# The last 3072 tokens of a pooled attention and feed-forward kernel: h for 768 tokens at a time from seven products of a 2x2 split, with w_in's combined weights made on VectorE and kept in DRAM

## The chip, the cores and the metric

The kernel runs on one core of a Trainium2 chip. The time is that of the device, in microseconds, from the start to the end of one execution. TensorE (PE) multiplies matrices and loads its weights (PEld) beside them; VectorE (DVE), ScalarE (ACT) and GpSimd (POOL) work element by element; SyncE (SP) issues the copies between DRAM and the on-chip memory.

## The reference

```python
def _attn_ref(q, k, v):                       # q, k, v: 8 batches, 8 heads, 576 tokens, 64
    k_p = k.reshape(B, H, 72, 8, D).mean(axis=3)
    v_p = v.reshape(B, H, 72, 8, D).mean(axis=3)
    scores = np.matmul(q, k_p.transpose(0, 1, 3, 2)) / np.sqrt(D)
    attn = np.exp(scores - scores.max(-1, keepdims=True))
    attn = attn / (attn.sum(-1, keepdims=True) + 1e-09)
    return np.matmul(attn, v_p)

def _moe_ref(x, w_in, w_out):                 # x: 4608 x 512, w_in: 512 x 2048, w_out: 2048 x 512
    h = x @ w_in
    g = h * np.clip(h + 3.0, 0.0, 6.0) / 6.0
    return g @ w_out
```

x is the attention's result, its heads side by side. All of it is in float32.

## The kernel before

**Precision.** A float32 number is kept as the sum of two numbers of a shorter format (`hi`, a rounded copy, and `lo`, what is left), and a product is three matmuls: hi by hi, lo by hi, hi by lo. So x, g, w_in, w_out, the attention weights and the pooled values all exist in two parts. Weights are scaled by 2^8 on the way.

**Blocks.** The 4608 tokens are worked on in blocks of 512, 256, 384, six times 512, and 384 tokens (`BLOCKS`). d_ff is cut into 16 slices f of 128. For a block, a `Step` for each f does:

- `h` (L775, matmuls L782): 12 matmuls, 4 slices of d_model by 3 products, as wide as the block, into one of two PSUM banks h0 and h1;
- `relu` (ScalarE, L790), `gate` (VectorE, L794, reads the bank again), `hi` (ScalarE, L798) and `lo` (VectorE, L802) make g in two parts;
- `out` (matmuls L812): for each 128 tokens three matmuls of 512 columns into the banks o0 to o3, which add up over all f. After the last f each bank is scaled, copied out and stored (L818, L819).

`run` (L1004) goes through the 16 steps of a block with a lag of two: `h` of step u, then `out` of step u-2. So between h of a step and its out, TensorE has two other h and two other out.

**Attention** for a block is a list of small steps (`block_steps`, L609): scores of a tile of 128 tokens and 4 heads (matmul L412, maximum L416 on VectorE, four exps L420 on ScalarE, division L448 and L454 on GpSimd), transposes (L518, L520) and the product with the pooled values (`av`, matmuls L583), whose result ScalarE copies to x (L585). Loads of q, k, v and the pooling of k and v (L214, L332, on VectorE) hang on these steps. `Paced.slot` hands out the steps of the next block between the matmuls of this one, so that x is complete before the next block begins; `split_x` (L556) then makes x's two parts.

**Order.** The tile framework derives the waits from what each instruction reads and writes. The order on each engine from the first load to the fourth step of block 1 is written out by hand (`ORDER`). Behind it a planner orders each engine's instructions when the program is built: first in the program comes first, among those that are ready in its own timeline. Engines then work in that fixed order, and so does SP's queue of copies.

**Weights.** All of w_in and w_out are loaded and split once during block 0 (`Prep`) and stay in the on-chip memory: 16 tiles w_f, each with w_in and w_out of one f in two parts.

Of the kernel before, what the change touches and what calls it, by code (L numbers as in the profile page):

```python
# [17 lines left out]
P = 128  # L18
# [3 lines left out]
BLOCKS = [512, 256, 384] + [512] * 6 + [384]  # L22
# [5 lines left out]

WSCALE = 2.0**8

# [45 lines left out]
def attention_moe_kernel(  # L76
# [50 lines left out]
    const = ctx.enter_context(tc.tile_pool(name="const", bufs=1))  # L127
    pool = ctx.enter_context(tc.tile_pool(name="pool", bufs=2))
    psum = ctx.enter_context(tc.tile_pool(name="psum", bufs=1, space=PSUM))

# [46 lines left out]
    def stage(i):  # L177

        if i % 2 == 0:
            stages.append(const.tile([P, 2, 2 * DM], F32, name="stage", tag=f"w_{NF - 2 - i // 2}"))  # L180
        return stages[-1][:, i % 2]
# [187 lines left out]
    def load_second():  # L369

        t = const.tile([P, 2, 2 * DM], F32, name="v1", tag=f"w_{NF - 2 - 6}")
# [172 lines left out]

    xs = {}

    def x_tile(j, name, dtype):
        if (j, name) not in xs:
            xs[j, name] = pool.tile([P, NCC, max(BLOCKS)], dtype, name=name, bufs=1)
        return xs[j, name][:, :, : BLOCKS[j]]  # L550

# [83 lines left out]
    w_in_hi, w_in_lo, w_out_hi, w_out_lo = {}, {}, {}, {}  # L635
    wraw, ubuf = {}, []
# [5 lines left out]
    def w_tile(name, f, a, b, shape, dtype):  # L642
        tag = f"w_{f}" if (a, b) == (0, 2) else f"w_{f}_{a}"
        return const.tile([P, b - a] + shape, dtype, name=f"{name}_{f}", tag=tag)
# [10 lines left out]
    class Prep:  # L655
# [10 lines left out]
        def __init__(self, f):  # L666
            self.f, self.made = f, {}
            if f < 2:
                ubuf.append(const.tile([P, 2 * DM], F32, name="u", tag=f"w_{NF - 1}_{1 - f}"))
# [34 lines left out]
        def place(self, part, n):  # L704

            f, (a, b, _, _) = self.f, part
            if a not in self.made:
                x, y = next(g for g in groups(f) if g[0] <= a < g[1])
                w = w_tile("w", f, x, y, [2, DM], F32R)
                for i in range(x, y):  # L710
                    self.made[i] = w, i - x
                    for m in range(2):
                        t = w[:, i - x, m]
# [35 lines left out]
    class Block:  # L749
# [3 lines left out]
        def sums(self, t):  # L753

            if t not in self.pos:
                banks = [self.banks[t]]
                if self.j == len(BLOCKS) - 1 and t == self.nt - 1:
                    banks.append(self.banks[t + 1])
                n = DM // len(banks)
                self.pos[t] = [  # L760
                    (slice(i * n, (i + 1) * n), psum.tile([P, DM], F32, name="pso", tag=b)[:, :n])
                    for i, b in enumerate(banks)
                ]
            return self.pos[t]
# [4 lines left out]
    class Step:  # L769
# [18 lines left out]
        def relu(self):  # L788
            self.g = pool.tile([P, max(BLOCKS)], F32, name="g", bufs=1)[:, : self.n]
# [6 lines left out]
        def hi(self):  # L796
            self.ghi = pool.tile([P, max(BLOCKS)], F32R, name="ghi", bufs=3)[:, : self.n]
            nc.scalar.copy(self.ghi, self.g)  # L798

        def lo(self):  # L800
            self.glo = pool.tile([P, max(BLOCKS)], F32R, name="glo", bufs=3)[:, : self.n]
            nc.vector.tensor_tensor(out=self.glo, in0=self.g, in1=self.ghi.bitcast(F32), op=ALU.subtract)  # L802

        def out(self, slot=no_slot, tiles=None):
            f, blk = self.f, self.blk
            for t in tiles or range(self.t0, self.t1):
# [3 lines left out]
                for cols, pos in blk.sums(t):  # L810
                    for i, (l, r) in enumerate(products):
                        nc.tensor.matmul(pos, l, r[:, cols], start=f == 0 and i == 0, stop=f == NF - 1 and i == 2)  # L812
# [4 lines left out]
                for (cols, pos), scaled in zip(blk.sums(t), (nc.scalar.mul, nc.vector.tensor_scalar_mul)):  # L817
                    scaled(o[:, cols], pos, 1.0 / WSCALE**2)  # L818
                    nc.sync.dma_start(out[at : at + P, cols], o[:, cols])  # L819


    ident = const.tile([P, P], F32, name="ident")
    make_identity(nc, ident)
    small = const.tile([P, 7], F32, name="small")
    mask, half = small[:, :6], small[:, 6:]
    nc.gpsimd.memset(half, 0.5)
    kbds = [const.tile([P, NPAIR, 2 * SP], F32, name=f"kbd{i}") for i in range(2)]
# [3 lines left out]
    nc.gpsimd.memset(half, 0.5)  # L831

    class Paced:


        def __init__(self, steps, n):
            self.steps, self.n, self.at, self.done = steps, n, 0, 0

# [4 lines left out]
        def upto(self, m):  # L843
            while self.done < m:
# [4 lines left out]
                if step:  # L849
                    step()  # L850

# [118 lines left out]
    def att_steps(j):  # L970

        if j == len(BLOCKS):
            return []
# [30 lines left out]
    def run(steps, lag, attention, first_slot=0, preps={}):  # L1004


        n_out = sum(x.t1 - x.t0 for x in steps[max(first_slot - lag, 0) : len(steps) - lag])
        paced = Paced(attention, len(steps) - first_slot + n_out - 4)
        for u in range(len(steps) + lag):
# [25 lines left out]
            if steps[0].blk.j == 1 and u == 3:  # L1035
                window.append(len(traced))
            if u == len(steps) - 1:
                paced.upto(len(attention))
                if attention:
                    split_x(steps[0].blk.j + 1)  # L1040
            if u >= len(steps) and steps[0].blk.j == len(BLOCKS) - 1:
                continue
            if u >= lag:
                steps[u - lag].out(slot)
        if steps[0].blk.j < len(BLOCKS) - 1:
            return

        mark = len(traced)
        for tiles in range(steps[0].blk.nt - 1), [steps[0].blk.nt - 1]:
            for x in steps[len(steps) - lag :]:  # L1050
                x.out(tiles=tiles)
        mine = [i for i in traced[mark:] if i.engine == mybir.EngineType.PE]
        for x, y in zip(mine, mine[1:]):
            behind(y, x.name)
# [3 lines left out]
    for j in range(1, len(BLOCKS)):  # L1058
        blk = Block(j, ["o0", "o1", "o2", "o3"])
        run([Step(blk, f, 0, blk.nt) for f in range(NF)], 2, att_steps(j + 1))  # L1060
# [44 lines left out]
```

## Time and profile before

| | |
|---|---|
| time, median of three runs | 921.4 us (921.24 to 921.76) |
| the profiled execution | a span of 920.7 us from its first to its last instruction |
| TensorE busy | 908.4 us, 99% |
| VectorE, ScalarE busy | 456.5 and 461.5 us, 50% each |
| GpSimd busy | 81.1 us, 9% |
| copies | 57.19 MB, 62 GB/s over the span |
| granted TensorE clock | full |

Busy time is a sum over the run; which engine sets the time is read from the chain that ended last and from the idle time before instructions. The spacing of matmuls, not their duration, is what one costs, since the next begins while the last is still draining.

### The profile page before, as it was taken

The page shows a single profiled execution, that of the slowest core. Times are in us where ns is not written, and L with a number is a line of the kernel's source. Part 1 is how long each engine was busy: PE and PEld are TensorE (multiplying, and loading weights), DVE is VectorE, ACT ScalarE, POOL GpSimd, SP SyncE. Part 2 cuts the span into 40 slices and gives each one's busy share as a digit, 9 for nine tenths or more (in the row PEclk, how much of TensorE's full clock was granted, in tenths as well). Part 3 has the DMA queues.
Part 4 walks back from the last instruction along what each step waited for, and adds up shares of the span by engine and source line. Part 5 has one row for each costly group of instructions (what it writes and reads, how often), then busy time and mean ns, then how long its engine had stood idle before and what let it go on. Part 6 is the DMA issues. An engine that isn't in the chain of part 4 may idle for free.

```text
span 920.7 us, 12711 instructions
## 1 busy us (share of the span) xinstructions
PE 908.4 (99%) x4568; PEld 777.6 (84%) x4568; DVE 456.5 (50%) x916; ACT 461.5 (50%) x1340; POOL 81.1 (9%) x167
## 2 busy tenths in 40 slices
PE   7899999999999999999999999999999999999998
PEld 6788889999888888888888888888888888888997
DVE  6999855475356333824356326633356224332322
ACT  5998665465355434633456335633545344333322
POOL 4100001021000100101011101110101001000000
PEclk9999999999999999999999999999999999999999
DMA  9970203050031002300042004200210000000100
GB/s 295 391 262 0 92 12 121 1 167 18 1 113 59 24 1 79 106 12 6 0 143 59 12 1 136 60 12 1 91 40 25 1 34 24 1 0 1 47 1 35
DMA packets 41935, 57.19 MB, mean 62 GB/s; under 512 B 7568, under 2 KB 23696, under 8 KB 41872
## 3 DMA queue, kind: packets, MB, share of 16 engines
q1 hardware_dynamic: 41728, 56.37, 19.0%
q8 instruction: 36, 0.59, 0.3%
q14 instruction: 27, 0.22, 0.1%
q10 hardware_dynamic: 144, 0.00, 0.0%
HBM read 46.93 MB, written 9.44 MB: 61 GB/s over the span
## 4 chain that ended last, share of the span: by engine, by line
PE 96%; DMA 3%; DVE 1%; issue 0%; SPq 0%; ACT 0%; ACTq 0%; DVEq 0%
PE pso L812 43%; PE psh L782 43%; PE psa L583 4%; PE psa L412 4%; PE psa L518 2%; DMA raw<-w_in_l 1%; DMA raw<-w_out_l 1%; DMA stage<-k_l 1%; PE psa L520 0%; SPq L257 0%; ACT stage L420 0%; DVE u L689 0%; DVE u L700 0%; DVE stage L448 0%; DVE a L510 0%
## 5 line engine op out<-in xcount | busy, mean ns | idle before, releaser
L782 PE MATMUL psh<-xhi,w 128*128 128x512 f32 (+2 forms) x1288 | 401.9, 372 | 0.0
L812 PE MATMUL pso<-w,ghi 128*128 128x512 f32 (+1 forms) x1184 | 367.0, 391 | 0.0
L782 PEld LDWEIGHTS psh<-xhi,w 128*128 128x128 f32 x1288 | 237.7, 188 | 36.1 <-issue 0.4
L812 PEld LDWEIGHTS pso<-w,ghi 128*128 128x128 f32 x1184 | 214.2, 188 | 36.0
L782 PE MATMUL psh<-xlo,w 128*128 128x512 f32 (+2 forms) x644 | 237.4, 369 | 0.0
L794 DVE SCALAR_TENSOR_TENSOR g<-g,psh 128x512 f32<-128x512 f32 (+2 forms) x161 | 101.3, 629 | 271.5 <-ACT g L790 270.3
L812 PE MATMUL pso<-w,glo 128*128 128x512 f32 (+1 forms) x592 | 225.9, 386 | 0.0
L790 ACT ACTIVATE g<-psh,small 128x512 f32<-128x512 f32 (+2 forms) x161 | 103.7, 644 | 208.7 <-PE psh L782 192.3
L782 PEld LDWEIGHTS psh<-xlo,w 128*128 128x128 f32 x644 | 121.2, 188 | 18.1
L802 DVE TENSOR_TENSOR glo<-g,ghi 128x512 fp32r<-128x512 f32 (+2 forms) x161 | 102.3, 635 | 62.0 <-ACT ghi L798 60.1
L812 PEld LDWEIGHTS pso<-w,glo 128*128 128x128 f32 x592 | 111.1, 188 | 21.7
L798 ACT CAST ghi<-g 128x512 fp32r<-128x512 f32 (+2 forms) x161 | 92.9, 577 | 70.0 <-DVE g L794 67.4
L420 ACT ACTIVATE e<-psa,mx 128x72 f32<-128x72 f32 x256 | 78.6, 322 | 50.6 <-DVE mx L416 49.9
L448 POOL TENSOR_TENSOR a<-e,sm 128x256 f32<-128x256 f32 x60 | 40.5, 675 | 513.5 <-PE pso L812 180.3
L420 ACT ACTIVATION_READ_ACCUMULATOR e<-psa,mx 128x1 f32 x256 | 52.9, 207 | 0.0
L416 DVE TENSOR_REDUCE mx<-psa 128x4 f32<-128x288 f32 x72 | 32.3, 453 | 29.5 <-PE psa L412 29.0
L412 PEld LDWEIGHTS psa<-kbd,qt 128*128 128x128 f32 x288 | 43.1, 189 | 4.2
L412 PE MATMUL psa<-kbd,qt 128*128 128x144 f32 x288 | 45.5, 285 | 0.0
L585 ACT COPY x<-psa 128x192 f32<-128x192 f32 (+7 forms) x60 | 22.9, 386 | 32.6 <-PE psa L583 32.4
L332 DVE TENSOR_REDUCE vsum<-vst 128x64 f32<-128x512 f32 (+1 forms) x36 | 37.7, 1065 | 2.6 <-DMA vst<-v_l 2.0
L436 DVE TENSOR_SCALAR sm<-sm 128x4 f32<-128x4 f32 x72 | 12.6, 178 | 48.9 <-ACT e L420 45.7
L529 ACT CAST ahi<-psa 128x256 fp32r<-128x256 f32 (+1 forms) x70 | 24.5, 352 | 18.7 <-PE psa L518 9.8
(93 smaller groups left out, 630.7 us busy)
## 6 DMA issues: line engine op xcount, KB each, us to landing
out<-o SPq DMA_DIRECT2D x35, 256.0 KB, 2.3
raw<-w_in_l SPq DMA_DIRECT2D x16, 512.0 KB, 8.5
raw<-w_out_l SPq DMA_DIRECT2D x16, 512.0 KB, 9.2
kst<-k_l SPq DMA_DIRECT2D x28, 288.0 KB, 3.0
qt<-q_l SPq DMA_DIRECT2D x28, 256.0 KB, 3.3
vst<-v_l SPq DMA_DIRECT2D x24, 256.0 KB, 3.1
vst<-vr_l SPq DMA_DIRECT2D x36, 64.0 KB, 1.9
stage<-k_l SPq DMA_DIRECT2D x4, 288.0 KB, 4.1
```

Source lines behind the costliest of these rows:

```text
L332: nc.vector.tensor_reduce(out=vs[:n, p], in_=st[:n, : POOL * D].rearrange("p (o d) -> p d o", o=POOL), axis=AX.X, op=ALU.add)
L412: nc.tensor.matmul(to, qt[:, p, :], kbds[b % 2][:, p, :], start=r == 0, stop=r == last)
L416: nc.vector.tensor_reduce(out=self.mx, in_=self.ps, axis=AX.X, op=ALU.max, negate=True)
L420: nc.scalar.activation(self.e[:, h], self.ps[:, h], AF.Exp, bias=self.mx[:, h : h + 1], accum_out=self.sm[:, h : h + 1])
L448: engine.tensor_tensor(out=self.a[:, : 4 * D].rearrange("p (h s) -> p h s", h=4), in0=e[:, :, :D], in1=sm[:, :, None].broadcast_to([P, 4, D]),
L583: nc.tensor.matmul(ps, l, r, start=n == 0, stop=n == len(mms) - 1)
L782: nc.tensor.matmul(self.ps, l[f][:, c, :], r[:, c, :], start=c == 0 and i == 0, stop=c == NCC - 1 and i == 2)
L790: nc.scalar.activation(self.g, self.ps, AF.Relu, bias=half, scale=1.0 / (6.0 * WSCALE))
L794: nc.vector.scalar_tensor_tensor(out=g, in0=g, scalar=1.0, in1=self.ps, op0=ALU.min, op1=ALU.mult)
L798: nc.scalar.copy(self.ghi, self.g)
L802: nc.vector.tensor_tensor(out=self.glo, in0=self.g, in1=self.ghi.bitcast(F32), op=ALU.subtract)
L812: nc.tensor.matmul(pos, l, r[:, cols], start=f == 0 and i == 0, stop=f == NF - 1 and i == 2)
```

## The change

The first four blocks have 512, 256, 384 and 384 tokens and are worked as before. The last 3072 tokens are worked in four super-blocks of 768 tokens, each two halves of 384 (`BLOCKS` lists the halves).

**h in seven products.** For two neighbouring slices of d_ff (a pair i, 8 pairs) and two halves of tokens, h is a 2x2 arrangement of results, each a sum of two products over the two halves of d_model. Winograd's form of Strassen's scheme computes it with seven products instead of eight: each takes one combination of w_in's four quarters and one of x's four quarters, 2 slices of 128 by 3 matmuls of 384 columns. Four combinations are made of w_in's quarters (product 7, 3, 5, 6), three quarters are used as they are (1, 2, 4); of x's quarters likewise. The products of neighbouring pairs are interleaved (`PERIOD`): 1, 2 of a pair, 7 of the pair before, 5, 6, then 4 of the pair before, 3. They add up in banks: X (one of h0, h1, o0 in turn) takes 1, then 6, 7 and 4 of a pair; Y (o1) takes 5 and 3; Z (o2) takes 2. In between ScalarE copies out what X and Y hold (`keep`, after 1, 5 and 6), and VectorE adds the copies (`plus`, after 2, 3 and 7). g for all 16 f of the super-block is kept.

**out afterwards.** When all of h is done, `split_g` splits g for one f after the other, and plain matmuls, 18 per f, add up six tiles of 128 tokens in six banks.

**Weights through DRAM.** In the steps of block 2, VectorE makes the combined quarters of w_in (`sums_of`, 16 calls, one per step), splits them with ScalarE, and eight copies of 64 KB store them to DRAM; `plain_of` (8 calls, every second step) stores three uncombined quarters of a pair and w_out of two f. In the super-blocks the weights are read back: for h in chunks of two products (512 KB, 28 chunks per super-block, four buffers, loads asked for three chunks ahead), for out one f at a time (512 KB, four buffers).

**x's combinations.** `x_ops` makes them with four sums on GpSimd and 14 pairs of a ScalarE copy and a VectorE subtraction: for the first super-block in the last steps of block 3, for the next ones during the last five f of out.

**Memory.** The tiles of w_0 to w_7 are given up in the middle of block 3 and taken by the x operands and the weight chunks; those of w_8 to w_15 after block 3, and taken by g, its parts and w_out.

**Attention.** Block 1 makes block 2's and half of block 3's; block 2 the other half and that of the first super-block's first half; block 3 that of its second half; each super-block that of the next, one half during h, one during out.

The diff, cut to its core:

```diff
-BLOCKS = [512, 256, 384] + [512] * 6 + [384]
+BLOCKS = [512, 256, 384, 384] + [384] * 8
+PLAIN = 4
+HALF = 384
+PERIOD = ((1, 0), (2, 0), (7, 1), (5, 0), (6, 0), (4, 1), (3, 0))
+RAW = {1: (0, 0), 2: (0, 1), 4: (1, 1)}
+CHUNK, NSTREAM, AHEAD, NC, NREL = 2, 4, 3, 6, 3
+TAIL = 5
+    N1 = [(i, o) for t in range(NPR + 1) for o, d in PERIOD for i in [t - d] if 0 <= i < NPR]
+    def sums_of(i, h):
+        half = slice(h * P, (h + 1) * P)
+        q = early[-1].tile([P, 4, P], F32, name="wq", bufs=2)
+        for r, w in enumerate(pair_of(i)):
+            nc.vector.tensor_tensor(
+                out=q[:, 2 * r : 2 * r + 2], in0=w[:, 0, :, half], in1=w[:, 1, :, half], op=ALU.add
+            )
+        for to, a, b, how in ((0, 0, 2, ALU.subtract), (2, 2, 3, ALU.add), (3, 3, 0, ALU.subtract), (1, 1, 3, ALU.subtract)):
+            nc.vector.tensor_tensor(out=q[:, to], in0=q[:, a], in1=q[:, b], op=how)
+        hi = early[-1].tile([P, 4, P], F32, name="wh", bufs=2)
+        nc.scalar.copy(hi.bitcast(F32R), q)
+        nc.vector.tensor_tensor(out=q.bitcast(F32R), in0=q, in1=hi, op=ALU.subtract)
+        for o, at in {7: 0, 3: 1, 5: 2, 6: 3}.items():
+            for m, t in enumerate((hi, q)):
+                nc.sync.dma_start(dram_of(i, o)[:, m, half], t[:, at])
+    def plain_of(i):
+        for o, (r, q) in RAW.items():
+            nc.sync.dma_start(dram_of(i, o), pair_of(i)[r][:, :, q])
+        for f in (2 * i, 2 * i + 1):
+            nc.sync.dma_start(w2_dram[f], w_of[f, 1].bitcast(F32))
+    def next_w(n):
+        while (m := len(loaded)) <= n // CHUNK + AHEAD and m < len(supers) * len(w_dram):
+            loaded[m] = late[0].tile([P, CHUNK, 2, 2 * P], F32R, name="ws", bufs=NSTREAM)
+            nc.sync.dma_start(loaded[m].bitcast(F32), w_dram[m % len(w_dram)])
+        return loaded[n // CHUNK][:, n % CHUNK]
+    def super_block(n, j, first_att, second_att):
...
+        for m, (i, o) in enumerate(N1):
+            if o == 1:
+                g_of[i] = late[1].tile([P, 4, HALF], F32, name=f"g{i}")
+                chain[i] = [bank(["h0", "h1", "o0"], i), bank(["o1"], i), bank(["o2"], i), {}]
+            X, Y, Z, kept = chain[i]
+            ps = {1: X, 2: Z, 3: Y, 4: X, 5: Y, 6: X, 7: X}[o]
+            w, t = next_w(n * len(N1) + m), ops[o]
+            paced.slot()
+            for c in range(2):
+                for k, (l, r) in enumerate(((0, 0), (0, 1), (1, 0))):
+                    nc.tensor.matmul(
+                        ps,
+                        w[:, l, c * P : (c + 1) * P],
+                        t[:, r, c],
+                        start=o in (1, 2, 5) and c == 0 and k == 0,
+                        stop=c == 1 and k == 2,
+                        skip_group_check=True,
+                    )
+            if o in (1, 5, 6):
+                kept[o] = keep(ps)
+            elif o == 2:
+                plus(i, 0, ps, kept[1])
+            elif o == 3:
+                plus(i, 2, ps, kept[6])
+            elif o == 7:
+                plus(i, 3, ps, kept[5])
+            elif o == 4:
+                gate(ps, i, 1)
...
+        for f in range(NF):
+            if f + 1 < NF:
+                split_g(f + 1)
+            w = next_w2(n * NF + f)
+            for t in range(NT2):
+                if f < NF - TAIL:
+                    paced.slot()
+                elif rest:
+                    rest.pop(0)()
+                hi, lo = (x[:, t * P : (t + 1) * P] for x in parts[f])
+                products = (hi, 0), (hi, 1), (lo, 0)
...
+                for cols, pos in sums[t]:
+                    for k, (l, r) in enumerate(products):
+                        nc.tensor.matmul(pos, l, w[:, r, cols], start=f == 0 and k == 0, stop=end and k == 2)
...
+    make = [lambda i=i, h=h: sums_of(i, h) for i in range(NPR) for h in range(2)]
+    plain = [lambda i=i: plain_of(i) for i in range(NPR)]
+    for n, step in enumerate(make):
+        hooks[2].setdefault(2 + n, []).append(step)
+    for n, step in enumerate(plain):
+        hooks[2].setdefault(2 + 2 * n, []).append(step)
+    hooks[3][NF // 2 + 1] = [swap]
+    for n, step in enumerate(x_ops(PLAIN)):
+        hooks[3].setdefault(12 + n // 3, []).append(step)
+    for j, mine, more, share in (
+        (1, att_steps(2), third[:cut], 1.0),
+        (2, third[cut:] + att_steps(4), (), 1.0),
+        (3, att_steps(5), (), 0.7),
+    ):
```

223 lines of the change are left out of this document (172 added, 51 removed).

## The prediction

> **What bounds the kernel now.** First the page: its span line and the busy time of each engine.
>
> ```profile
> span 920.7 us, 12711 instructions
> PE 908.4 (99%) x4568; PEld 777.6 (84%) x4568; DVE 456.5 (50%) x916; ACT 461.5 (50%) x1340; POOL 81.1 (9%) x167
> PE 96%; DMA 3%; DVE 1%; issue 0%; SPq 0%; ACT 0%; ACTq 0%; DVEq 0%
> PE pso L812 43%; PE psh L782 43%; PE psa L583 4%; PE psa L412 4%; PE psa L518 2%; DMA raw<-w_in_l 1%; DMA raw<-w_out_l 1%; DMA stage<-k_l 1%; PE psa L520 0%; SPq L257 0%; ACT stage L420 0%; DVE u L689 0%; DVE u L700 0%; DVE stage L448 0%; DVE a L510 0%
> ```
>
> TensorE is busy for 99% of the span and is 96% of the chain that ended last; half of that is h (L782), half out (L812). VectorE and ScalarE stand at 50%. So matmuls taken away count in full, until another engine stops feeding TensorE. A matmul's mean duration overlaps its neighbours; what one costs is its spacing, which the chain in order of time shows in unbroken runs.
>
> ```profile
> 428.86 2.75 PE psh L782 x12
> 451.13 5.44 PE pso L812 x24
> 900.67 2.11 PE psh L782 x12
> ```
>
> Twelve h matmuls of 512 columns take 2.75 us (0.2292 each), twelve of 384 columns 2.11 (0.1758), 24 out matmuls 5.44 (0.2267). Then I cut the span where a block's first h matmul starts: block 1 (256 tokens), block 2 (384), two blocks of 512, and what the copy queue did at the busy start.
>
> ```profile
> 125.30:183.60 58.30, 58.30 (x372) 53.10 (x371) 29.51 (x78) 33.66 (x115) 8.03 (x16) 1.00 0.17 53
> 183.60:259.50 75.90, 75.90 (x404) 68.89 (x403) 41.05 (x92) 40.78 (x136) 8.27 (x18) 1.00 0.20 56
> 259.50:357.50 98.00, 98.00 (x467) 81.93 (x466) 46.46 (x96) 46.23 (x145) 8.55 (x18) 1.00 0.16 46
> 357.50:456.00 98.50, 98.50 (x470) 82.36 (x469) 46.40 (x92) 46.16 (x142) 9.32 (x19) 1.00 0.16 47
> 0.00:23.00 23.00, 16.48 (x109) 15.21 (x110) 13.97 (x32) 13.23 (x49) 9.64 (x23) 1.00 0.96 295
> 38.00:42.00 4.00, 4.00 (x28) 3.62 (x27) 4.00 (x7) 3.38 (x8) 0.00 (x0) 1.00 1.03 410
> ```
>
> The columns after the length are PE, weight loads, DVE, ACT, POOL, clock, DMA share, GB/s. The clock is full. A 512 block is 98.5 us of TensorE: 192 h (44.0) and 192 out (43.5), so attention for 512 tokens costs it 11.0.
>
> **The saving.** Before, the tokens from 1152 on take 6 x 192 h matmuls of 512 columns and 192 of 384; after, 192 plus 4 x 56 products x 6 = 1344, all of 384. 1152 x 0.2292 = 264.0 against 1344 x 0.1758 = 236.3: **27.7 us less**. Out matmuls are the same number. Attention keeps its tiles, and its value products fall into 12 pieces either way (cut at blocks and batches), so it only moves: 192 tokens of block 3's to block 1 (8 us more of a VectorE that is half idle there), the rest one super-block ahead. The end keeps its form, the last tile in two banks with two copies and two stores. With nothing late the span is 893.0.
>
> The Trainium skill, "TensorE: Matmul & The Clock Gate", section Back-to-back issue gap, gives a warm gap of N/2.4 + 2.5 ns, 215.8 and 162.5 ns; by it the saving would be an estimated 30.2. Our rows have some 13 ns more at either width, so the rows decide.
>
> **VectorE in block 2.** The combined weights of 16 half chunks are made there, one per step of block 2 or its tail. Prices:
>
> ```profile
> L802 DVE TENSOR_TENSOR glo<-g,ghi 128x512 fp32r<-128x512 f32 x111 | 76.7, 691 | 41.0 <-ACT ghi L798 39.8 <-PE psa L583 0.8
> L794 DVE SCALAR_TENSOR_TENSOR g<-g,psh 128x512 f32<-128x512 f32 x111 | 76.1, 686 | 200.7 <-ACT g L790 199.7
> L798 ACT CAST ghi<-g 128x512 fp32r<-128x512 f32 x111 | 69.1, 623 | 49.5 <-DVE g L794 48.7
> L802 DVE TENSOR_TENSOR glo<-g,ghi 128x256 fp32r<-128x256 f32 x18 | 7.7, 430 | 7.2 <-ACT ghi L798 6.6 <-PE psa L583 0.5
> L530 DVE TENSOR_TENSOR alo<-psa,ahi 128x128 fp32r<-128x128 f32 x14 | 3.9, 283 | 1.2 <-ACT ahi L529 1.2
> L802 DVE TENSOR_TENSOR glo<-g,ghi 128x384 fp32r<-128x384 f32 x32 | 17.8, 556 | 13.7 <-ACT ghi L798 13.7
> L794 DVE SCALAR_TENSOR_TENSOR g<-g,psh 128x384 f32<-128x384 f32 x32 | 17.7, 552 | 59.5 <-ACT g L790 59.4
> L790 ACT ACTIVATE g<-psh,small 128x384 f32<-128x384 f32 x32 | 18.6, 582 | 42.8 <-PE psh L782 39.6 <-DVE glo L802 2.1 <-DVE sm L437 1.1
> L585 ACT COPY x<-psa 128x384 f32<-128x384 f32 x12 | 5.7, 479 | 5.0 <-PE psa L583 4.9
> L562 DVE TENSOR_TENSOR xlo<-x,xhi 128x512 fp32r<-128x512 f32 x24 | 15.0, 684 | 0.0
> ```
>
> One sums step is two adds of 256 (0.430), four of 128 (0.283) and a subtraction of 512 (0.691): 2.68 us, 16 of them 42.9. Attention for 512 tokens is 46.40 - 16 x (0.691 + 0.686) - 4 x 0.684 = 21.6 of VectorE; block 2 now prepares 576 tokens instead of 512, 2.7 more, and 1.4 more of TensorE. VectorE: 41.05 + 42.9 + 2.7 = **86.7 us against TensorE's 77.3**, over by 9.4. Behind a sums step stand the gates of the next h, on an engine that works in order. Cover: h(u)'s bank is needed again after two outs and an h, 2 x 2.04 + 2.11 = 6.2, less relu and gate (1.1): 5.1. So 4.3 to 9.4 reach TensorE if the sums keep their places, 0 if the planner lets them slip into block 3, whose VectorE has room (86.7 less the sums is 44 of 77). I take 7, since the sums stand ahead of the next gate in program order and are ready at once. ScalarE's 16 copies of 0.62 fit under the idle half.
>
> **The stores behind it.** Eight stores of 64 KB follow each sums step, and five larger ones each pair: 168 issues, 23.1 MB (8.4 + 6.3 + 8.4), on SP's queue, ahead of the loads of k, v and q.
>
> ```profile
> 0.74 1.81 SPq L257 DMA_DIRECT2D stage<-k_l  x4
> 4.62 0.47 SPq L260 DMA_DIRECT2D stage<-vr_l  x1
> vst<-vr_l SPq DMA_DIRECT2D x36, 64.0 KB, 1.9
> kst<-k_l SPq DMA_DIRECT2D x28, 288.0 KB, 3.0
> stage<-k_l SPq DMA_DIRECT2D x4, 288.0 KB, 4.1
> stage<-vr_l SPq DMA_DIRECT2D x4, 128.0 KB, 8.9
> raw<-w_in_l SPq DMA_DIRECT2D x16, 512.0 KB, 8.5
> ```
>
> An issue takes 0.45 us (1.81 / 4). Per step: eight (3.6), half of five (1.2) and about one load (0.5): 5.3. The two buffers of a sums step come free when its stores land, so a sums step repeats no faster than (3.3 with its ScalarE copy + 5.3 + landing)/2: 5.3 us for a landing of 1.9, inside VectorE's own 5.42 per step; 5.8 for 3.0; 6.35 for 4.1; 8.75 for 8.9. Over 14 repeats that adds 0, 5, 13 and 47 us if VectorE waits in order, and 0 if the planner has put gates before the sums that aren't ready. The copy engines: 47 GB/s at share 0.16 is 294 per full share, 410 at 1.03 is 398, so 23.1 MB take 0.76 to 1.02 of block 2's 77 us beside the 0.20 that is there. That is close to full; I take 5.
>
> The Trainium skill, "DMA: Bandwidth & Descriptors", Specifications, names 512 B as the least transfer for line rate, and these stores have 512 B rows; at its 435 GB/s they would take an estimated 53 us, and this term nothing. The mixed loads' 294 per full share speak against it.
>
> **Inside a super-block.** Phase A (h): seven products of 1.055 us per pair, 7.4. Per pair ScalarE has three copies (0.48) and four relus (0.58), 3.8; VectorE three adds and four gates, 3.9; attention for 384 tokens adds 16 us of VectorE (21.6 x 3/4) over the eight pairs, 2.0 each. Both stay near 70%, but what was two steps of cover shrinks: product 4 accumulates into the bank that VectorE must first have added from after product 7, two products (2.1 us) earlier; product 3 waits so for a ScalarE copy of product 5. Less 0.56 of work and a hand-over, some 1.4 us are free. Longest occupants now:
>
> ```profile
> 476.69 3.03 DVE L332 TENSOR_REDUCE vsum<-vst 128x64 f32<-128x512 f32 x3
> L420 ACT ACTIVATE e<-psa,mx 128x72 f32<-128x72 f32 x256 | 78.6, 322 | 50.6 <-DVE mx L416 49.9
> ACT g L790 <- PE psh L782: 192.3, 94, 4.3
> L790 ACT ACTIVATE g<-psh,small 128x512 f32<-128x512 f32 (+2 forms) x161 | 103.7, 644 | 208.7 <-PE psh L782 192.3
> L448 POOL TENSOR_TENSOR a<-e,sm 128x256 f32<-128x256 f32 x60 | 40.5, 675 | 513.5 <-PE pso L812 180.3 <-DVE sm L437 157.8 <-PE psa L520 94.2
> SPq L193 <- PE psa L412: 198.0, 19, 27.0
> ```
>
> A single reduction (about 1.0) and four exps (1.3) fit; three reductions in a row are 1.6 late. 2304 tokens of attention lie in super-blocks, four batches of six reductions, half of them in phase A: four such runs, 6.5 us; none if they are spread; 18 if each of 24 pairs loses 0.75. In 94 of 161 relus ScalarE sat waiting for TensorE, so answers are mostly prompt. I take 4.
>
> Weights: a 512 KB chunk per two products, 248 GB/s of 398, asked for three chunks (6.3 us) ahead: 1.3 of transfer and 1.9 of landing fit. Phase B (out) splits g one f (4.1 us) ahead: a cast and a subtraction of 768, under the 0.62 + 0.69 of 512 doubled. The 14 x splits (7.2 us of ScalarE, 7.8 of VectorE) and four POOL mixes of 768 (some 2 us each, three times 0.675) have five f's, 20 us. Only the first w_out loads of the first phase B start late: 1. Super-blocks' ends copy banks under 2 us of remaining matmuls: nothing, else 0.6 x 4.
>
> **Sum**: -27.7 + 7 + 5 + 4 + 1 = -10.7; span 910.0. The runs' median is 921.4, 0.7 above the profiled span, so **911 us** (910.7).
>
> **Rivals.**
> *All hidden.* The planner lets sums slip and places attention between deadlines; only 1 to 6 us of the 27.7 are lost: 895 to 900, centre 896. For it: 50% idle on both helpers over the whole run. Against: the 86.7 in one block. Chance 0.28.
> *Slower: the stores set block 2's pace.* VectorE waits in order for buffers whose stores are late, gates stand behind it, TensorE follows. It decides from 16 us in 14 repeats: landing 4.6. Half way between 4.1 and 8.9, at 6.5, a step is 7.55, 30 us more than now: 921.4 - 27.7 + 12 + 30 = 936. For it: the 0.96 share of the start, with those landings. Against: 1.9 to 3.0 otherwise, and the planner. Chance 0.17.
> *Phase A stumbles.* Each pair loses 0.75 us, and weights are queued behind SP's waits for q buffers (up to 27 us now, where nothing else was due); +18 instead of 4: 925. At 8.5 us per landing, three in flight, each of 112 chunks would even be 0.7 late, 80 us; those loads stood in a long queue, these don't. Chance 0.10.
> The forecast, 903 to 919, has 0.45.
>
> **Numbers.** About 0.2% either way is what can be told from no change: 919.6 to 923.2. Faster is the first rival, the forecast less its edge (0.44): 0.72; slower, most of the last two, 0.21; same 0.07. The range 895 to 932 leaves out 0.08 below (the fastest of all hidden) and 0.10 above; the forecast's own is 903 to 919.
>
> **What will show it.** h matmuls of 384 columns at 0.176 spacing, 1536 from token 1152 on; phase A near 67 us with attention and 59 without, phase B 74 and 66. Block 2 longer than 77 with VectorE full there means the sums; VectorE idle there, released by stores, means the rival. Gaps of TensorE in phase A put down to VectorE or ScalarE price the third term; those put down to the weights' loads are the chunk stream. I am wrong if block 2 keeps its length, or if phase A's products are spaced above 1.1 us throughout.

## The result and the profile after

The changed kernel takes **930.4 us** (median of four runs, 929.34 to 931.31) against 921.5 for the kernel before on the same chip: a ratio of 1.0093, 95% interval 1.0079 to 1.0107. It is 0.9% slower. 911 was forecast.

From the page of the changed kernel: the span, the busy times, the chain's shares by engine, the granted clock in 40 slices, and the stream of combined weights (copies, KB each, median us from issue to landing).

```profile
span 927.5 us, 14141 instructions
PE 892.9 (96%) x4760; PEld 800.6 (86%) x4760; DVE 577.6 (62%) x1167; ACT 514.8 (55%) x1473; POOL 115.9 (12%) x184
PE 75%; DVE 12%; DMA 6%; SPq 3%; ACT 3%; issue 2%; DVEq 0%; ACTq 0%
PEclk9999999999999997999999999999999999999999
ws<-wd SPq DMA_DIRECT2D x112, 512.0 KB, 4.2
```

TensorE's busy time fell by 15.5 us, and yet the span grew by 6.8: TensorE went from 99% to 96% of the span and from 96% to 75% of the chain. One slice, from 348 to 371 us, has a lower clock. No other engine is busy for more than 62%.

Next the stages, cut where their first matmul starts: blocks 1, 2 and 3, then phase A (h) of the first, second and fourth super-block and phase B (out) of the fourth. The columns are those of the prediction's windows.

```profile
125.20:188.80 63.60, 61.30 (x389) 55.06 (x387) 38.14 (x99) 39.46 (x151) 10.68 (x22) 1.00 0.76 267
188.80:265.80 77.00, 74.69 (x392) 68.14 (x392) 65.50 (x169) 43.02 (x137) 8.31 (x16) 0.98 0.55 164
265.80:345.70 79.90, 78.87 (x426) 71.33 (x427) 47.60 (x119) 43.93 (x146) 9.85 (x18) 1.00 0.31 97
345.70:448.50 102.80, 92.46 (x502) 87.33 (x502) 75.94 (x160) 67.72 (x223) 21.13 (x31) 0.93 0.70 222
510.50:591.10 80.60, 78.55 (x452) 75.57 (x451) 58.52 (x129) 55.86 (x189) 10.72 (x21) 1.00 0.77 257
796.40:866.50 70.10, 70.10 (x390) 67.38 (x389) 32.28 (x59) 30.90 (x59) 0.00 (x0) 1.00 0.63 204
866.50:923.70 57.20, 55.79 (x285) 47.15 (x283) 14.22 (x16) 12.98 (x17) 0.00 (x0) 1.00 0.36 123
```

The first phase A stands out: 102.8 us where the second takes 80.6, at a mean clock of 0.93. To compare stages that hold different work I multiplied each stage's matmuls by their undisturbed spacing (0.174 us for 384 columns, 0.227 for 512; attention's by their own medians) and took the result from the stage's length. What is left is the stage's loss:

| us | before | after |
|---|---|---|
| matmuls at undisturbed spacing | 894.9 | 866.5 |
| loss in block 0 | 16.7 | 16.8 |
| block 1 | 0.3 | 2.9 |
| block 2 | 0.7 | 5.4 |
| block 3 | in the next row | 2.6 |
| first super-block | 4.8 for blocks 3 to 9 | 18.6 |
| the other three super-blocks | | 11.0 |
| after the last matmul | 3.3 | 3.8 |
| span | 920.7 | 927.5 |

The matmuls became 28.4 us cheaper, as forecast; lost time grew by 35, half of it at one place. That place, in the timeline of the changed kernel around the first super-block's start (start, us, engine and line; in brackets the idle time before and what ended it):

```profile
353.79 0.84 ACT L614 COPY x<-psa 128x384 f32<-128x384 f32 x2
353.80 1.22 PE L1024 MATMUL psx<-x,ws 128*128 128x384 f32 x6
354.70 1.82 POOL L954 TENSOR_TENSOR mid<-x 128x768 f32<-128x768 f32 x1
356.60 2.00 POOL L954 TENSOR_TENSOR x<-x 128x768 f32<-128x768 f32 x1
356.86 2.15 DVE L946 TENSOR_TENSOR x<-x,x 128x384 fp32r<-128x384 f32 x1
358.93 0.44 DVE L439 TENSOR_REDUCE mx<-psa 128x4 f32<-128x288 f32 x1
359.47 0.32 ACT L443 ACTIVATE e<-psa,mx 128x72 f32<-128x72 f32 x1 [4.02 <-DVE mx L439]
360.84 1.33 PE L435 MATMUL psa<-kbd,qt 128*128 128x144 f32 x4 [4.84 <-ACT e L443]
365.82 2.29 PE L1024 MATMUL psx<-x,ws 128*128 128x384 f32 x6 [1.31 <-DVE x L946]
369.05 1.97 PE L1024 MATMUL psx<-x,ws 128*128 128x384 f32 x5 [0.94 <-DVE x L946]
```

The super-block begins at 345.7, but the last pieces of x for its second half (block 5) are copied until 354.6, nine us later. Only then can GpSimd mix and VectorE split the combinations that products 3 to 7 need (1 and 2 take quarters of block 4's x as they are). TensorE first waits 4.84 us in attention's scores, which stand in that stretch: their maxima (`mx`) are taken on VectorE behind the first split, 2.15 us long, which needs block 5's x. Then it waits 1.31 and 0.94 us for split x. And the clock drops: six matmuls (one product) took 1.22 us at 353.8, and 2.29 at 365.8. The trace's clock record has half clock from 360.9 to 374.5, 13.7 us.

### The profile page after: what moved, and what is told of

Its sections match the earlier page's. It is cut to its first block, busy times and chain, and to the rows that moved or that the text cites. A ratio compares the mean times of both kernels' runs of the same rounds, so it can differ in the third digit from the quotient of the medians.

```text
span 927.5 us, 14141 instructions
## 1 busy us (share of the span) xinstructions
PE 892.9 (96%) x4760; PEld 800.6 (86%) x4760; DVE 577.6 (62%) x1167; ACT 514.8 (55%) x1473; POOL 115.9 (12%) x184
## 4 chain that ended last, share of the span: by engine, by line
PE 75%; DVE 12%; DMA 6%; SPq 3%; ACT 3%; issue 2%; DVEq 0%; ACTq 0%
PE psx L1068 27%; PE psx L1024 20%; PE psh L806 11%; PE pso L836 11%; PE psa L612 3%; PE psa L435 2%; DMA vst<-v_l 2%; DVE vsum L355 2%; DMA out<-o 1%; PE psa L541 1%; SPq L911 1%; DVE g L994 1%; ACT e L443 1%; DMA kst<-k_l 1%; DVE x L946 1%
## 5 line engine op out<-in xcount | busy, mean ns | idle before, releaser
L1024 PE MATMUL psx<-x,ws 128*128 128x384 f32 x1344 | 257.2, 342 | 5.9 <-ACT c L1004 2.7
L1024 PEld LDWEIGHTS psx<-x,ws 128*128 128x128 f32 x1344 | 234.5, 190 | 12.0 <-ACT c L1004 3.7
L1068 PE MATMUL psx<-ws,ghi 128*128 128x512 f32 (+1 forms) x800 | 237.4, 385 | 2.0 <-DVE g L994 1.8
L1068 PEld LDWEIGHTS psx<-ws,ghi 128*128 128x128 f32 x800 | 145.9, 188 | 29.1 <-DVE g L994 2.6
L806 PE MATMUL psh<-xhi,w 128*128 128x384 f32 (+2 forms) x520 | 147.5, 342 | 4.1 <-ACT xhi L590 3.0
L1068 PE MATMUL psx<-ws,glo 128*128 128x512 f32 (+1 forms) x400 | 148.3, 383 | 0.0
L836 PE MATMUL pso<-w,ghi 128*128 128x512 f32 x384 | 122.2, 399 | 0.5 <-ACT ghi L822 0.5
L806 PEld LDWEIGHTS psh<-xhi,w 128*128 128x128 f32 x520 | 94.1, 190 | 12.3 <-ACT xhi L590 3.4
L806 PE MATMUL psh<-xlo,w 128*128 128x384 f32 (+2 forms) x260 | 88.3, 339 | 0.9 <-DVE xlo L591 0.9
L836 PEld LDWEIGHTS pso<-w,ghi 128*128 128x128 f32 x384 | 69.2, 188 | 11.6 <-ACT ghi L822 0.7
L814 ACT ACTIVATE g<-psh,small 128x384 f32<-128x384 f32 (+2 forms) x65 | 37.5, 577 | 31.1 <-PE psh L806 19.7
```

The lines of the kernel that those rows point to most:

```text
L806: nc.tensor.matmul(self.ps, l[f][:, c, :], r[:, c, :], start=c == 0 and i == 0, stop=c == NCC - 1 and i == 2)
L836: nc.tensor.matmul(pos, l, r, start=f == 0 and i == 0, stop=f == NF - 1 and i == 2)
L1024: nc.tensor.matmul(ps, w[:, l, c * P : (c + 1) * P], t[:, r, c], start=o in (1, 2, 5) and c == 0 and k == 0, stop=c == 1 and k == 2, skip_ ...
L1068: nc.tensor.matmul(pos, l, w[:, r, cols], start=f == 0 and k == 0, stop=end and k == 2)
```

## The experiments

Theory one was the prediction's own second and third terms: VectorE's sums and their stores delay everything behind them. Theory two: block 5's x is late, because attention is. Each kernel below differs from the changed kernel by the edit shown. Ratios are to the kernel before on the same chip; 0.001 is 0.9 us. A stage's row is from one execution, and executions of one kernel differ by some us (none_big's five from 926.2 to 931.9, its profile being the fastest).

**The sums' arithmetic left out, two ways of storing.**

```diff
 def sums_of(i):                      # none_big: 32 stores of 256 KB; hooks at 2 + 2 * n
-    ...
+    for n, o in enumerate((7, 3, 5, 6)):
+        nc.sync.dma_start(dram_of(i, o), pair_of(i)[n // 2][:, :, n % 2])
 def sums_of(i, h):                   # none_small: 128 stores of 64 KB
-    ...
+    for n, o in enumerate((7, 3, 5, 6)):
+        for m in range(2):
+            nc.sync.dma_start(dram_of(i, o)[:, m, half], pair_of(i)[n // 2][:, m, n % 2, half])
```

> The sums of w_in's quarters are left out: nothing of them is computed on VectorE or ScalarE, and in their place uncombined quarters are stored, with 32 copies of 256 KB instead of 128 of 64 KB (so h is not the reference's). All else as in the changed kernel (930.4 us). Theory 'debt': the sums and their stores in blocks 2 and 3 hold up the attention, whose x for the second half of the first super-block is late, and TensorE stands at that super-block's start; without them the 18.6 us lost in it shrink to under 6 and blocks 1 and 2 lose some 5 less: 908 to 914. Rival 'density': attention for 1536 tokens is packed into blocks 1 to 3 and is late anyway: 924 to 930.

> The arithmetic of the sums is left out (uncombined quarters are stored, h is not the reference's), but their 128 stores of 64 KB stay on SP's queue as they are. If it is VectorE's work that holds the attention up: 908 to 916, like the run without either. If it is the queue, in which the loads of k, v and q stand behind these stores: 923 to 930.

Measured: none_big 929.7 us, 1.0076 [1.0050, 1.0101]; none_small 939.1, 1.0182 [1.0165, 1.0199]. Block 2 and the first phase A of none_big, then block 2 of none_small:

```profile
189.00:263.30 74.30, 73.66 (x391) 67.05 (x391) 34.02 (x74) 34.40 (x111) 4.70 (x11) 1.00 0.61 203
342.40:446.20 103.80, 93.52 (x506) 87.87 (x505) 75.51 (x162) 67.96 (x225) 21.05 (x31) 0.92 0.66 220
```

```profile
190.70:287.60 96.90, 82.88 (x420) 75.14 (x421) 46.35 (x111) 45.03 (x164) 10.43 (x24) 0.91 0.64 202
```

Without the sums block 2's loss falls from 5.4 to 1.9, but the first phase A is a microsecond longer: the last copies of x start at 352.5, 1.6 us earlier than with the sums, while the super-block starts 3.3 earlier. So theory one fails as it stood: what block 2 gets back is waited for again. With small stores that nothing spaces (none_small, slower than either of its two expectations), VectorE is idle for half of block 2 and yet the block takes 96.9 us. There VectorE waits for loads of v in a queue of stores, and TensorE for what stands behind that on VectorE:

```profile
197.25 1.01 DVE L355 TENSOR_REDUCE vsum<-vst 96x64 f32<-96x512 f32 x1 [6.66 <-DMA vst<-vr_l]
198.78 0.69 PE L806 MATMUL psh<-xlo,w 128*128 128x384 f32 x1 [7.44 <-DVE xlo L591]
260.91 1.01 DVE L355 TENSOR_REDUCE vsum<-vst 128x64 f32<-128x512 f32 x1 [9.80 <-DMA vst<-v_l]
262.44 0.69 PE L806 MATMUL psh<-xhi,w 128*128 128x384 f32 x1 [5.16 <-DVE g L818]
```

So a long queue of copies by itself can hold TensorE up.

**Larger sums and stores.** Half as many instructions and stores for the same result.

```diff
-    q = early[-1].tile([P, 4, P], F32, name="wq", bufs=2)
+    q = early[-1].tile([P, 4, 2 * P], F32, name="wq", bufs=1)      # hi likewise
 ...
-                nc.sync.dma_start(dram_of(i, o)[:, m, half], t[:, at])
+                nc.sync.dma_start(dram_of(i, o)[:, m], t[:, at])
```

> The sums are made for a whole pair at a time: 8 instructions twice as wide instead of 16 per pair, 34 us of VectorE instead of 43, and 64 stores of 128 KB instead of 128 of 64 KB; one buffer of each kind instead of two of half the size. Same result. 'Queue' and 'debt' both: the loads get through earlier, 916 to 924. 'Density': 928 to 931. If the single buffers make VectorE wait for the stores: above 931.

Measured 927.2 us, 1.0054 [1.0036, 1.0072]: 3 to 4 us better than the change, between the expected ranges. The first super-block's loss is 15.1.

**Is it the late x?** In same_x the first super-block's combinations read block 4's x for both halves; in delay the program hands out no attention during its first ten products.

```diff
-            return lambda: x_tile(j + k, "x", F32)[:, 2 * h : 2 * h + 2]
+            return lambda: x_tile(j + (k if j > PLAIN else 0), "x", F32)[:, 2 * h : 2 * h + 2]   # same_x
-            paced.slot()
+            if n or m >= 10:                                                                     # delay
+                paced.slot()
```

> The first super-block's combinations of x take the first half's x (block 4, ready 47 us earlier) in place of the second half's (block 5) too, so its h is not the reference's; the attention for block 5 is still computed. All else as in the changed kernel (930.4 us, 18.6 us lost in the first super-block). Theory 'late x': the loss at the first super-block's start is the wait for block 5's x: it falls below 7 us, 916 to 921, and TensorE's clock stays full there. Rival 'crowd': VectorE, ScalarE and GpSimd are too full there whatever x waits for: 926 to 931.

> In the first super-block alone, no attention step is handed out before the eleventh product, so the pooling of v (which stands in VectorE's order ahead of the last parts of x and waits for loads that wait for stores of block 3) comes later. If that order makes most of the loss at the start: 918 to 924, and TensorE's clock stays full there. If x itself is late: 928 to 932.

Measured: same_x 923.7 us, 1.0021 [1.0008, 1.0034]; delay 930.6, 1.0092 [1.0073, 1.0110]. The first phase A of same_x:

```profile
347.20:434.30 87.10, 84.51 (x489) 81.32 (x488) 60.96 (x130) 58.50 (x186) 12.54 (x23) 1.00 0.77 259
```

87.1 us instead of 102.8, at full clock; the super-block's loss is 8.2 instead of 18.6. The time lies between the two expectations. So the late x costs 7 to 10 us there. delay says nothing on the attention that stands in that stretch, because it didn't put it off: the planner filled the same scores in at the same place, and TensorE's matmuls from the super-block's start on have the same order and the same four waits (4.84, 0.70, 1.31 and 0.94 us) as in the changed kernel. Whether those scores elsewhere would save part of the 4.84 us stays untested.

**What happens around the gaps.** busy adds 24 matmuls that serve nothing ahead of the fifth product, to keep the clock up; mix_dve has VectorE instead of GpSimd mix x.

```diff
+            if n == 0 and m == 4:                                                                # busy
+                idle2 = psum.tile([P, DM], F32, name="idle2", tag="o3")
+                for _ in range(24):
+                    nc.tensor.matmul(idle2[:, :HALF], ops[2][:, 0, 0, :P], ops[2][:, 0, 0], start=True, stop=True)
-                nc.gpsimd.tensor_tensor(out=to(), in0=p(), in1=q(), op=how)
+                nc.vector.tensor_tensor(out=to(), in0=p(), in1=q(), op=how)                      # mix_dve
```

> 24 matmuls of 384 columns into a bank that nothing else uses (4.2 us at full clock) stand ahead of the fifth product of the first super-block, where TensorE sat idle for 4.8 us and then had half its clock for 13.7. If the idle time brought the half clock on and it cost some 6 us: the clock stays full there and the time falls to 923 to 927. If the half clock has another cause, or costs nothing since TensorE waits then anyway: 930 to 935.

> The four sums of x's quarters per super-block are made on VectorE instead of GpSimd, where one takes 1.8 to 2.1 us and VectorE's own sums beside it take as long instead of 0.55. If that blocking costs at the first super-block's start: 1.0 us per sum on VectorE instead of 2, 4 to 6 us less in all, 925 to 927. If x's lateness alone sets it: 929 to 931.

Measured: busy 931.9 us, 1.0112 [1.0097, 1.0127]; mix_dve 929.9, 1.0090 [1.0075, 1.0105]. In busy, gaps of 3.06, 2.13 and 2.11 us remain, with 6.8 and 3.4 us at half clock, so it doesn't price the clock. mix_dve can't be told from the change.

**Why x is late.** Three tries to bring attention forward: carry lets its steps run on from one block's list into the next; no_store leaves out the sums and all but three of the stores, and every load of weights reads those three again; store_act issues the stores from ScalarE's queue.

```diff
-            later_steps[j] = block_steps(j)                                                      # carry
-            every += later_steps[j]
+        ...  # one list: scores of the next tile while the last one's transposes and products follow
+            later_steps[j] = every[done[j - 1] : done[j]]
-        for o, (r, q) in RAW.items():                                                            # no_store
+        if i == 0:
 ...
-                nc.sync.dma_start(dram_of(i, o)[:, m, half], t[:, at])                           # store_act
+                nc.scalar.dma_start(dram_of(i, o)[:, m, half], t[:, at])
```

> The list of attention steps from block 3 on is one pipeline: the scores of the next block's first tiles are put between the last transposes and value products of this one, where each block's list ran empty before the next began. Same work, same result. Theory 'late x' by 'serial lists' (each list of 384 tokens takes 45 to 70 us from its first score to its last value product, four of them stand before the first super-block, and blocks 1 to 3 have 220 us): block 5's x comes some 15 us earlier and 8 to 15 us of the loss go: 915 to 923. Rival 'density' (the helpers' work itself is too much for these blocks): 927 to 932.

> The making of the weights is left out whole: no sums, and of the stores to DRAM only three (one chunk and one w_out slice), which all loads of the super-blocks read again (h and out are not the reference's). If the stores (40 large ones, pulled into block 1 by the planner, and 128 small ones) hold up the loads of v, k and q, and so the attention and the first super-block: 912 to 918, with block 5's x some 15 us earlier. If attention is late without them ('steps in a row': each of its steps waits for one of two PSUM banks in turn): 925 to 929.

> All 168 stores of weights are issued from ScalarE's queue instead of SP's, so that loads of k, v and q don't stand behind them. Same result. If SP's queue was what held the loads up: 920 to 926. If ScalarE, which now spends some 0.4 us on each issue (60 us over blocks 1 to 3, where it is busy for 126 of 220 us), holds its own work up more than that: above 933.

Measured: carry 936.9 us, 1.0157 [1.0137, 1.0176]; no_store 918.6, 0.9961 [0.9946, 0.9976], 0.6 above the range of its first theory; store_act 951.5, 1.0307 [1.0290, 1.0324]. carry's last copy of x starts at 360.4, later still, and it is slower than either expectation. store_act's block 0 loses some 35 us instead of 17: the planner puts stores there, ahead of ScalarE's own work. Without sums and stores block 5's x comes 14 us earlier:

```profile
L614 ACT COPY x<-psa x4: 479/480/481, 333.0 to 339.6; 128x384 f32<-128x384 f32 x4
```

**A third bank.** In blocks 1 to 3 attention's products go in turn through two PSUM banks. The bank o3 is not used there, since these blocks have two or three tiles of 128 tokens. banks gives it to attention in these blocks; banks_all does so in the phases A as well.

```diff
             if j == 1 and u == 3:
                 window.append(len(traced))
                 paced.add_more()
+                att_banks[:] = ["a1", "a0", "o3"]
 ...
+    att_banks[:] = ["a1", "a0"]
     for n, j in enumerate(supers):
```

> Attention takes its PSUM banks in turn from three instead of two, in blocks 1 to 3 alone (o3 is free there, since these blocks have two or three tiles of 128 tokens). Same work, same result. 'Steps in a row' (the list's steps follow each other through two banks, some 3 us each, whatever the engines' load): block 5's x comes 10 us or more earlier, and the time falls to 916 to 923. If loads or the helpers' work set the attention's pace: 928 to 932.

> As before with three banks, and in the super-blocks' h phases too, where o3 is free as well. 'Steps in a row': 1 to 4 us below the run with three banks in blocks 1 to 3 alone, 913 to 921. Otherwise as that run, within 1 us.

Measured: banks **919.5 us**, 0.9976 [0.9960, 0.9992]; banks_all 922.7, 1.0014 [1.0002, 1.0026]. Attention's scores and transposes up to 346 us (count, least/median/most ns, first and last start), and the copies of x from 300 us on, in the changed kernel:

```profile
L435 PE MATMUL psa<-kbd,qt x100: 283/286/299, 125.6 to 331.5; 128*128 128x144 f32 x100
L541 PE MATMUL psa<-ident,a x48: 270/272/299, 141.3 to 344.4; 128*128 128x128 f32 x48
L614 ACT COPY x<-psa x8: 310/390/480, 302.4 to 354.1; 128x192 f32<-128x192 f32 x4, 128x384 f32<-128x384 f32 x4
```

The same rows with the third bank, and its first phase A:

```profile
L435 PE MATMUL psa<-kbd,qt x100: 283/286/390, 125.4 to 293.3; 128*128 128x144 f32 x100
L541 PE MATMUL psa<-ident,a x48: 270/272/330, 141.1 to 310.3; 128*128 128x128 f32 x48
L614 ACT COPY x<-psa x4: 473/480/482, 316.6 to 323.6; 128x384 f32<-128x384 f32 x4
350.00:439.00 89.00, 85.54 (x488) 82.24 (x488) 65.66 (x150) 61.56 (x210) 12.18 (x26) 0.98 0.77 256
```

The same number of scores and transposes (100 and 48) ends 38 and 34 us earlier, block 5's x is complete 26 us ahead of its super-block instead of 9 us behind its start, and the loss there falls from 18.6 to 6.5. Two lines of code take 11 us off, and the kernel is 2 us faster than the one before. Block 2 now holds 102 of attention's matmuls where the changed kernel has 74, none_big 63 and no_store 87: the bank lets more of attention through there than taking sums or stores away does. Which single wait on a bank is the one that counts wasn't taken apart: the planner orders every engine anew. And banks_all, expected below banks, is 3 us above it; why is open.

**Do sums and stores cost anything once x is early?** Each of these has the third bank: banks_nosums with none_big's edit, banks_big with big's, banks_delay with delay's, banks_big_delay with both.

> The third bank, and the combined weights' arithmetic left out: 32 uncombined pieces are stored in their place, so the output is not the reference's. Theory A (the forecast's 7 us for VectorE's sums is not in the run): within 1.5 us of the run with three banks, 918 to 920. Theory B (with attention out of the way, VectorE's 42.9 us of sums show): 3 to 7 us faster, 912 to 916, and block 2's loss goes from 5.5 to about 2.

> The third bank and the pair-wise sums with 64 stores of 128 KB together; the output is the reference's. Theory A (what delays attention is its chain of steps through two banks, and the stores only add waits while that chain is tight): with the third bank block 5's x is complete some 25 us before the first super-block either way, so the larger stores bring at most 1 us on the run with three banks: 918.5 to 920. Theory B (the two causes are separate, and their gains add): 11 us from the bank and 3 from the larger stores: 916 to 917.

> The third bank, and no attention step during the first ten products of the first super-block; the output is the reference's. In the run with three banks one gap of 2.96 us of TensorE is left at the first super-block's start (366 us), behind scores that wait for VectorE, which waits for a load of v. Theory A (the chain from an output's store over a v load to VectorE's pooling): scores stand later than the load, the gap goes, and with it 3.4 us at half clock, 1.7 of loss: 914.5 to 916. Theory B (the planner sets the order anyway, the gap only moves): 918.5 to 920.5.

> All three edits together; the output is the reference's. If the first super-block's gap goes and the larger stores give their 3 us: 912 to 914. If neither adds to the third bank: 918.5 to 920.5.

Measured: banks_nosums 911.8 us, 0.9889 [0.9876, 0.9901]; banks_big **916.8**, 0.9944 [0.9930, 0.9957]; banks_delay 918.3, 0.9960 [0.9949, 0.9972]; banks_big_delay 917.3, 0.9950 [0.9939, 0.9962]. Block 2 with the third bank, with and without the sums:

```profile
190.00:272.30 82.30, 79.26 (x429) 71.34 (x430) 71.56 (x191) 48.87 (x161) 10.23 (x20) 1.00 0.53 156
```

```profile
188.90:264.70 75.80, 75.80 (x408) 69.22 (x409) 43.39 (x101) 40.40 (x141) 8.33 (x18) 1.00 0.62 205
```

Now taking the sums out, and with them 96 of the 128 small stores, brings 8 us (0.0087 of the ratio), where without the bank it brought 1.6 (0.0017, inside the intervals); block 2's loss falls from 5.5 to 1.4 and block 3's from 2.8 to 0.9. The second theory of these expectations holds: the causes are separate, but the cost of sums and stores hid behind the late attention. How the 8 us divide between VectorE's work and the number of stores isn't shown. Larger stores bring 3 us on top of the bank, and banks_big is the fastest of the kernels that leave nothing out: 5.3 us faster than the one before. banks_delay removes the last long gap, 2.80 us of TensorE in the trace of banks, and its half clock, but the super-block still loses 6.2 instead of 6.5: small waits take its place, and its gain can't be told from none. banks_delay and banks_big_delay lie in none of their expected ranges.

## Why the prediction was wrong

**The saving: right.** 27.7 forecast, 28.4 by the matmuls' spacing. The super-blocks' lengths came close too: with attention 142.8 us (67 + 74 forecast), without 127.3 (59 + 66). Phase A alone is longer than forecast, 80.6 and 70.1, and B shorter, because the planner puts the first out matmuls into A: 390 matmuls in the last phase A, 336 of them h.

**"So it only moves": the step that failed.** Attention was costed at nothing by its amount, not by its due time. The trace of before had what was needed. There, x for tokens 768 to 2176 was made between block 1's start at 125.3 and block 4's at 357.5: 1408 tokens in 232 us, 6.1 per us. The change needs x for 768 to 2304 between 125.2 and 345.7: 1536 in 220, or 7.0 per us, 15% faster, while sums and stores are added to the same blocks. VectorE had room (65.5 of 77 us busy in block 2, 47.6 of 79.9 in block 3); a chain of steps that follow each other through two banks, with loads in a queue of stores, did not go faster for that. The third bank shows the first cause (11 us), taking sums and stores away the second (12 us; the two overlap, since either makes x early enough). Of the 19.7 us between forecast and result late attention so accounts for some 11; the other 8 or 9 lie in the terms below and in part stay open.

**"Inside a super-block", 4 us.** The first super-block loses 18.6, the other three 11.0, where blocks 3 to 9 lost 4.8. The place was priced, its cause was not: no pair stumbles over reductions or late weights throughout, but the first one has no x. Of the 18.6, 12 went with the third bank. What makes up the other 6.5, and the 3 to 4 us of each later super-block, stays open.

**VectorE in block 2, 7 us.** Near in size, wrong in effect. The planner let part of the sums slip into block 3 (5 of their 16 last subtractions stand there), and VectorE had 65.5 us in block 2 and not 86.7; still block 2's loss rose by 4.7. Its length hardly moved, 77.0 us after 75.9, which the prediction had named as a sign that it is wrong. Where attention sets the end the term is worth nothing to 1.6 us; where it doesn't, sums and small stores together are worth 8. Terms were added that lie one behind the other: time given back in block 2 was lost again at the next wait.

**The stores, 5 us.** Not by the way that was priced: the copy engines' share in block 2 is 0.55, far from full. Nor by buffers of the sums (that rival had 936): the small stores land in 1.7 us in the median, and VectorE and ScalarE wait 1.2 and 1.0 us for them in blocks 2 and 3. none_small shows stores that stand ahead of attention's loads; in the changed kernel itself VectorE waits only 8.2 us for loads of k and v from block 1 to 3, so there this way isn't shown. Halving the stores' number, and that of the sums' instructions, gives 3 us with and without the bank. That sums and stores were priced at 12 and no_store is 12 faster is luck: no_store's x comes early too, and it is still some 19 us above what the forecast gives without these two terms (3.6 us saved, not 22.7).

**Not priced at all.** Block 2 now starts with a wait: x's first part is copied by ScalarE only behind block 1's last output banks (a copy of 1.12 us for two at 187.20): 2.1 us, with 3.4 at half clock behind it.

```profile
188.77 0.61 PE L806 MATMUL psh<-xhi,w 128*128 128x384 f32 x2 [2.13 <-ACT xhi L590]
190.28 0.69 PE L806 MATMUL psh<-xlo,w 128*128 128x384 f32 x1 [0.90 <-DVE xlo L591]
```

And the runs' time stands 1.8 us above the profiled span (929.34 and 927.5), not 0.7.

**The rivals.** "Phase A stumbles", 925, had the place and, by luck, nearly the time, but not the mechanism. "The stores set block 2's pace" is what none_small shows, in a kernel that has no sums to space its stores.

## What to carry to other kernels

When work is moved ahead, set its amount against its due time: tokens per microsecond that a chain of small steps has been seen to deliver, not the busy share of its engines. Where such a chain goes through few banks or buffers in turn, try one more before anything else. And a term that takes nothing off when it is removed may still cost its full price behind a later wait: measure it again once that wait is gone.

## What was not expected of the hardware

**The clock falls after some short gaps.** In the changed kernel a gap of 2.13 us at 188.8, with one of 0.90 behind it, was followed by 3.4 us at half clock, one of 4.84 us with three smaller ones behind it by 13.7; its gaps of 1.1 to 1.5 us alone by none. But the length of a gap doesn't decide it: gaps of 2.12 us in none_big (at 189.0) and 2.10 in banks_big (at 280.5) were followed by no half clock, and one of 1.34 us in banks_all (at 190.5, with 0.30 behind it) by 3.4 us of it. What decides stays open. Between the start and the end of the runs looked at, half clock lasted about 3.4, 6.8, 10.2, 13.7 or 17.1 us, steps of 3.4. The Trainium skill, "TensorE: Matmul & The Clock Gate", Part 1, has half clock after one idle window of about 3.4 us; the step agrees with these runs, but here gaps of 1.34 and 2.13 us were followed by it. The six matmuls above, 1.22 us and 2.29, show what it takes.

**GpSimd's sums stretch VectorE's.** Splits of x on VectorE, and the mixes of 768 on GpSimd, between 345 and 450 us (busy time and mean ns), in the changed kernel (first its row for the whole run: count, least/median/most ns) and then with the mixes on VectorE:

```profile
L946 DVE TENSOR_TENSOR x<-x,x x48: 528/548/2150, 315.4 to 787.1; 128x384 fp32r<-128x384 f32 x48
```

```profile
L946 DVE TENSOR_TENSOR x<-x,x 128x384 fp32r<-128x384 f32 x12 | 9.9, 863 | 0.0
L954 POOL TENSOR_TENSOR x<-x 128x768 f32<-128x768 f32 x2 | 3.8, 1904 | 0.1
```

```profile
L946 DVE TENSOR_TENSOR x<-x,x 128x384 fp32r<-128x384 f32 x12 | 7.0, 610 | 0.0
L954 DVE TENSOR_TENSOR x<-x 128x768 f32<-128x768 f32 x2 | 1.9, 946 | 0.0
```

In the whole run of the changed kernel these splits take 528 ns at least, 548 in the median and 2150 at most, as at 356.86 beside GpSimd's sum; in mix_dve none takes more than 894. The Trainium skill, "GPSIMD Engine Reference", section 1. Specifications, says that GpSimd shares its SBUF interfaces with VectorE and contends with instructions that have two SBUF inputs; the trace agrees. Here it cost nothing that the time of mix_dve can tell.
